# Global value rows of batch 1 written by VectorE; casts of batch 2's global rows placed behind batch 1's first pair

## The chip, the cores and the metric

The kernel runs on one core of one Trainium2 chip. The metric is the device time of one execution in microseconds (us); the figure for a kernel is the median of several runs. Engines are named as in the profile: PE is TensorE, DVE is VectorE, ACT is ScalarE, POOL is GpSimd, SP is SyncE, which issues most transfers.

## What is computed

A sliding-window attention with eight global tokens, and behind it a two-layer expert with a squared Relu:

```python
def _attn_ref(q, k, v, global_idx):          # q, k, v: 8 batches, 8 heads, 576 tokens, 64
    scores = scale * np.matmul(q, k.transpose(0, 1, 3, 2))
    mask = np.abs(pos[:, None] - pos[None, :]) <= 32
    mask = mask | is_global[:, None] | is_global[None, :]   # 8 global tokens
    scores = np.where(mask, scores, -1000000000.0)
    attn = softmax(scores)
    return np.matmul(attn, v)

def _moe_ref(x, w_in, w_out):                # x: 4608 x 512, w_in: 512 x 2048
    h = x @ w_in
    r = np.maximum(h, 0.0)
    return (r * r) @ w_out
```

Inputs and output are float32; the kernel computes in float16 with float32 sums.

## The kernel before

**Attention.** The heads of a batch are taken in four pairs, so that there are 32 pairs in all (`unit(i, ...)`, i = 4 * batch + pair). The 576 tokens stand in five key tiles of 120 tokens, and in front of each tile's tokens stand the eight global keys, so a tile has 128 rows. A pair is worked in two halves of its queries (`half`): scores (L617), Exp on ScalarE (L626), a multiplication with the mask on VectorE (L629), and the matmuls with the values (L653, L662), whose sums are divided (Ln and Exp of the negative, L685 and L686) and written into `xT` (L715), from which the expert reads. What the global queries add up to is kept apart (`gsh`, L703) and is spread over the eight global columns of `xT` by eight small copies per batch (`scatter`, L734).

**Value tiles.** `vb0` and `vb1` hold the values of even and odd batches. In partitions 0 to 7 of each of the five tiles stand the value rows of the global tokens (`vb[b][0:NG, x, ...]`), in the partitions behind them the tokens' rows, which POOL's queue fetches (`fetch_values`, L113). The global rows get there in three ways: for batch 0 VectorE casts them from `gv0` and copies them five times (`v_globals`, L447 and L449); for batches 1 and 2 VectorE casts both batches' rows at once into `g16s["v"]` (`values_in_place`, L368), and SP issues five transfers per batch from there (`value_globals`, L431); from batch 3 on they come from a gather through device memory (`gscr`). The float32 rows for batches 0 to 2 were fetched by SP at the start (`fetch_globals`, `grows`).

**Queries and keys.** Those of batches 0 and 1 are transposed on TensorE (`tr_k`, `tr_q`, L458 to L500). From batch 2 on they are laid out in scratch memory (`scr_k`, `scr_q`): tokens by nine transfers of POOL (`tokens_to_scratch`, L410), the eight global rows by one transfer each of SP (`globals_to_scratch`, L391; for batch 2 from `g16s["k"]` and `g16s["q"]`, which VectorE casts in `next_in_place`, L376). Two transposing transfers of SP bring them into `kb` and `qb` (`transposes`, L422). A one-element copy into `pin` on POOL (L846 for batch 2) holds POOL's token transfers back until something of the batch before has been written.

**Order.** There is no scheduler: each engine runs its instructions in the order in which the code records them, and SP and POOL issue transfers in that order too. Expert work stands in a list, `queue`, as pieces: `mm1_half` and `mm1` (L533, L514; a Relu, and a square on VectorE, L545 and L520) and `mm2` (L577; an evacuation L554 and an output store L556). `take(n)` records the next n pieces; `unit` does so between its own steps, after the scores, between the halves and at the end. In batch 1 a unit also transposes the next pair.

Around the change the order is: the last work of batch 0, `scatter(0, 1)`, `values_in_place()`, the rest of the queue, then everything that prepares batch 2, then the four units of batch 1. Each transfer and each reader of a tile waits for what the tile framework finds it to depend on.

Of the kernel before, what the change touches and what calls it, by code (L numbers as in the profile page):

```python
# [9 lines left out]
FP16 = mybir.dt.float16  # L10
# [37 lines left out]
def kernel(  # L48
# [11 lines left out]
    B, H, S, D = q.shape  # L60
    NG = global_idx.shape[0]
# [16 lines left out]
    def sbt(name, shape, dtype, bufs=1, tag=None):  # L78
        return sb.tile(shape, dtype, name=name, tag=(tag or name), bufs=bufs)
# [8 lines left out]
    pool, dve, act = nc.gpsimd, nc.vector, nc.scalar  # L88
# [5 lines left out]
    vb = {0: sbt("vb0", [P, NT, 2 * H, D], FP16)}  # L94
    w_in = sbt("w_in", [P, NDM, dff], FP16)
    w_out = sbt("w_out", [P, NFF, dm], FP16)
    XOFF = 36
    xT = sbt("xT", [P, NDM, XOFF + B * S], FP16)
# [13 lines left out]
    def fetch_values(b, x, hs=slice(0, H)):  # L112
        pool.dma_start(  # L113
            out=vb[b][NG : NG + KN[x], x, 2 * hs.start : 2 * hs.stop : 2],
            in_=v[b, hs, x * KT : x * KT + KN[x]].rearrange("h s d -> s h d"),
        )
# [44 lines left out]
    rows = sbt("rows", [P, 2], FP16)  # L161
# [25 lines left out]
    def clear_ones(op, t, tiles=range(NT)):  # L187
        for x in tiles:
            op(t[:, x, 1 : 2 * H : 2].bitcast(FP32), ONES)
# [144 lines left out]
    def gathered(nm, b):  # L334
        n = NG * H
        return gst[(nm, b // 2 - 1)][(b % 2) * n : (b % 2) * n + n]
# [3 lines left out]
    def store_rows(nm, b):  # L340
        gscr[(nm, b)] = dram.tile([NG, H * D], FP16, name=f"gscr_{nm}{b}")
        nc.sync.dma_start(
            out=gscr[(nm, b)].rearrange("g (h d) -> (g h) d", d=D), in_=gathered(nm, b)
        )

    grows = sbt("grows", [NG, 7, H, D], FP32, bufs=2, tag="gt")
    grow = {nm: grows[:, 2 * i : 2 * i + 2] for i, nm in enumerate("kqv")}
    gv0 = grows[:, 6]
    g16s = {nm: sbt("g16s" + nm, [NG, 2, H, D], FP16) for nm in "kqv"}

    def fetch_globals():
        _, at = nc.values_load_multi_w_load_instructions(
# [11 lines left out]
                    in_=src[nm][1:3, :, ds(at[g], 1), :].rearrange("b h o d -> o b h d"),  # L364
                )

    def values_in_place():
        dve.tensor_copy(out=g16s["v"], in_=grow["v"])  # L368
        value_globals(1)

    def globals_in_place(nm):
        act.copy(out=nat[nm][TP : TP + NG, :, TJ - 1], in_=grow[nm][:, 0])

    def next_in_place():
        for nm in "kq":
            dve.tensor_copy(out=g16s[nm][:, 1], in_=grow[nm][:, 1])  # L376

    def globals_to_scratch(b):
        for nm in "kq":
            rows, n, pitch, off = {"k": (KW, NT, P, 0), "q": (QW, 4, GRP, GTOK)}[nm]  # L380
            if (nm, b % 2) not in scr:
                scr[(nm, b % 2)] = dram.tile([rows, H * D], FP16, name=f"scr_{nm}{b % 2}")
                if nm == "k":
                    nc.sync.dma_start(
                        out=scr[("k", b % 2)][(NT - 1) * P + 8 + KN[-1] : KW],
                        in_=idle[0 : P - 8 - KN[-1]],
                    )
            t = scr[(nm, b % 2)]
            dst = t.rearrange("(x r) (h d) -> x r h d", x=n, d=D)[:, off : off + NG]
            if b == 2:  # L390
                nc.sync.dma_start(  # L391
                    out=dst.rearrange("x g h d -> g x (h d)"),
                    in_=g16s[nm][:, 1].rearrange("g h d -> g (h d)").unsqueeze(1).to_broadcast(
                        (NG, n, H * D)
                    ),
                )
                continue
            nc.sync.dma_start(
                out=dst.rearrange("x g h d -> (g h) x d"),
                in_=gathered(nm, b).unsqueeze(1).to_broadcast((NG * H, n, D)),  # L400
            )
        if b > 2:
            store_rows("v", b)

    def tokens_to_scratch(b):
        for nm in "kq":
            n, step, pitch, off = {"k": (NT, KT, P, NG), "q": (4, GTOK, GRP, 0)}[nm]
            for x in range(n):
                lo, hi = x * step, min((x + 1) * step, S)
                pool.dma_start(  # L410
                    out=scr[(nm, b % 2)][x * pitch + off : x * pitch + off + hi - lo].rearrange(
                        "s (h d) -> s h d", d=D
                    ),
                    in_=src[nm][b, :, lo:hi].rearrange("h s d -> s h d"),
                )

    def transposes(b):
        for nm, d_, w in (("k", kb, KW), ("q", qb, QW)):
            if not d_:
                d_["all"] = sbt(nm + "b", [P, 2, NHP, w], FP16, tag="st" + nm)  # L420
            d_[b] = d_["all"][:, b % 2]
            nc.sync.dma_start_transpose(out=d_[b], in_=scr[(nm, b % 2)][:, :])  # L422

    def values(b):
        t = vb[b]
        for x in range(NT):
            fetch_values(b, x)

    def value_globals(b):
        for x in range(NT):  # L430
            nc.sync.dma_start(  # L431
                out=vb[b][0:NG, x, 0 : 2 * H : 2],
                in_=gscr[("v", b)].rearrange("g (h d) -> g h d", d=D)
                if b > 2
                else g16s["v"][:, b - 1],
            )

    def cast_tokens(op, nm, hp):
# [4 lines left out]

    gv16 = sbt("gv16", [NG, H, D], FP16)

    def v_globals():
        dve.tensor_copy(out=gv16, in_=gv0)  # L447
        for x in range(NT):
            dve.tensor_copy(out=vb[0][0:NG, x, 0 : 2 * H : 2], in_=gv16)  # L449

    def transposed(nm, i, tag):
        b, hp = divmod(i, NHP)
# [143 lines left out]
    def take(n):  # L596
        for _ in range(min(n, len(queue))):
            fn, a = queue.pop(0)
            fn(*a)

    gsum = {}
    pin = sbt("pin", [P, 1], FP32)
# [8 lines left out]
    def scores(i, half, tag, wins):  # L611
        kt, qt = key_query(i)
        sc = pst(tag, [P, 2, 512])
        for t, so, c0, w in wins[half]:
            for e in range(2):
                r = slice(64 * e, 64 * e + 64)
                nc.tensor.matmul(  # L617
                    sc[:, e, so : so + w], kt[r, t, :], qt[r, c0 : c0 + w],
                    start=True, stop=True, skip_group_check=True,
                )  # L620
        return sc

    def weights(half, sc, wins):
        W = sum(x[3] for x in wins[half])
        et = sbt("et", [P, 2, SCW[0]], FP16, bufs=4)
        act.activation(  # L626
            out=et[:, :, 0:W], in_=sc[:, :, 0:W], func=AF.Exp, bias=0.0, scale=scale
        )
        dve.tensor_tensor(  # L629
            out=et[:, :, 0:W], in0=et[:, :, 0:W],  # L630
            in1=mask[:, MB[half] : MB[half] + W].unsqueeze(1).to_broadcast((P, 2, W)),
            op=ALU.mult,
        )
        return et
# [94 lines left out]
    def scatter(b, part=None, pairs=slice(0, NHP)):  # L729
        lo, hi = {  # L730
            None: (XOFF + b * S, XOFF + (b + 1) * S), 0: (0, HS + 1), 1: (XOFF, XOFF + S),
        }[part]
        for g in range(NG):
            dve.tensor_copy(  # L734
                out=xT[:, pairs, lo:hi][:, :, ds(gvs[part][g], 1)],
                in_=gxs[b][:, pairs, g : g + 1],
            )
# [29 lines left out]
    def half0(i):  # L767
        tag = pair_tag[i % 2]
        ets[i] = weights(0, scores(i, 0, tag, WIN), WIN)
# [26 lines left out]
        fetch_values(1, x)  # L796
    for j in range(4):
        pool.dma_start(out=w_out[:, ts(j, 4), :], in_=wo[:, ts(j, 4), :])
    v_globals()
    half0(2)  # L800
    keep_warm(SCHED["w6"])
    half0(3)
# [36 lines left out]
    tr_k(NHP, tag="tr")  # L839
    tr_q(NHP, tag="mm", op=act.copy)  # L840
    scatter(0, 1)
    values_in_place()
    take(99)
    next_in_place()
    globals_to_scratch(2)
    pool.tensor_copy(out=pin[0:1], in_=xT[0:1, 0, XOFF + 256 : XOFF + 257])  # L846
    tokens_to_scratch(2)
    transposes(2)
    vb[2] = vb[0]
    values(2)  # L850
    value_globals(2)
    queue += units[1] + units[2]

    def unit(i, n, nxt=None):
        scs = [scores(i, half, pair_tag[half], WIN2) for half in range(2)]
        et = [weights(half, scs[half], WIN2) for half in range(2)]
        take(n[0])
        if nxt:
            tr_k(nxt, tag="tr", tail=act.copy)
            tr_q(nxt, tag="mm", op=act.copy)  # L860
        for half in range(2):
            acc = outputs(i, half, et[half], pair_tag[half], WIN2, columns=i < 2 * NHP)
            finish_outputs(i, half, acc, columns=i < 2 * NHP)
            if half == 0:
                take(n[1])
        if i % NHP == NHP - 1:
            scatter(i // NHP)
        take(n[2])

    for hp in range(NHP):  # L870
        unit(NHP + hp, SCHED["b1"][hp], NHP + hp + 1 if hp + 1 < NHP else None)
        if hp == 2:
            clear_ones(dve.memset, vb[0])
            index_base()
# [51 lines left out]
```

## Time and profile before

| | us |
|---|---|
| median of 7 runs | 334.35 |
| lowest, highest | 334.0, 335.47 |
| profiled execution, its own time | 334.32 |
| span of the profiled execution | 332.5 |
| PE, busy in the span | 318.9 (96%) |
| DVE, busy | 228.8 (69%) |
| ACT, busy | 210.9 (63%) |
| POOL, busy | 106.5 (32%) |

Batch 0 takes the span up to about 34, batch 1 runs from there to 73, and batches 2 to 7 follow at about 33 each; the rest is expert work alone. The profile is of one execution. Its page gives busy time per engine, the span in 40 slices, queues, the chain of work that ended last, and groups of instructions by line and tile; the trace behind it can be asked for the order of instructions on an engine, with the idle time before each and what ended that.

### The profile page before, as it was taken

To read this page: it belongs to the slowest core of one execution; us is meant where nothing else is said; L and a number is where in the kernel's file an instruction comes from. 1 tells how busy PE (TensorE), PEld (TensorE's weight loads), DVE (VectorE), ACT (ScalarE), POOL (GpSimd) and SP (SyncE) were. 2 spreads that over 40 slices of the span, in tenths; PEclk is the share of its full clock that TensorE was granted. 3 is DMA by queue.
4 is the path that set the end of the run, shared out by engine and by line. 5 is a ranking of instruction groups with operands and counts; after the bars stand their busy time and mean duration, and the time that the engine had idled before them with its cause. 6 is when DMAs were issued, how large, how long until landed. Compare 5 with 4: busy or idle time off the path is not lost.

```text
span 332.5 us, 6922 instructions
## 1 busy us (share of the span) xinstructions
PE 318.9 (96%) x2427; PEld 166.0 (50%) x2427; DVE 228.8 (69%) x678; ACT 210.9 (63%) x416; POOL 106.5 (32%) x138
## 2 busy tenths in 40 slices
PE   8899489999999999999999999999999999999995
PEld 3558366545445454545454545454544444444444
DVE  7787936788868875888588858885888585323421
ACT  3879436559954995499549954995499536404700
POOL 9734635008940590059305900590000000000000
PEclk9999959999999999999999999999999999999999
DMA  8999999935999699489966998899710001011012
GB/s 182 178 204 181 173 188 143 157 110 72 149 140 134 99 144 153 117 109 135 138 137 101 144 143 124 110 146 122 138 65 0 34 32 64 2 63 63 2 53 73
DMA packets 148716, 37.59 MB, mean 113 GB/s; under 512 B 136658, under 2 KB 144202, under 8 KB 148682
## 3 DMA queue, kind: packets, MB, share of 16 engines
q0 software_dynamic: 105168, 17.93, 74.2%
q1 hardware_dynamic: 43368, 19.10, 31.4%
q8 instruction: 19, 0.31, 0.4%
q14 instruction: 15, 0.12, 0.2%
q10 hardware_dynamic: 146, 0.13, 0.1%
HBM read 37.31 MB, written 17.05 MB: 164 GB/s over the span
## 4 chain that ended last, share of the span: by engine, by line
PE 82%; DVE 7%; DMA 4%; ACT 3%; issue 2%; SPq 2%; DVEq 0%
PE mm L577 26%; PE mm L514 25%; PE tr L514 9%; PE tr L577 6%; PE mm L533 3%; PE sc L662 3%; PE acc L662 3%; PE sc L617 2%; DVE xT L734 2%; PE acc L617 2%; DMA vb<-g16sv 2%; DMA grows<-in_v_dram 2%; SPq L357 2%; ACT rec L686 1%; DVE xT L715 1%
## 5 line engine op out<-in xcount | busy, mean ns | idle before, releaser
L577 PE MATMUL mm<-w_out,gt 128*128 128x512 f16 x448 | 104.4, 379 | 0.0
L514 PE MATMUL mm<-xT,w_in 128*128 128x512 f16 x384 | 90.1, 379 | 0.8 <-DVE xT L734 0.8
L577 PEld LDWEIGHTS <-gt 128*128 128x128 f16 x560 | 52.5, 98 | 58.7
L514 PEld LDWEIGHTS <-w_in 128*128 128x128 f16 x512 | 47.5, 98 | 53.9 <-issue 1.0
L519 ACT ACTIVATE rl<-mm 128x512 f16<-128x512 f32 x96 | 54.8, 600 | 26.0 <-PE mm L514 25.3
L520 DVE TENSOR_TENSOR gt<-rl 128x512 f16<-128x512 f16 x128 | 52.1, 423 | 16.7 <-ACT rl L519 14.5
L626 ACT ACTIVATE et<-sc 128x880 f16<-128x880 f32 (+1 forms) x32 | 28.9, 902 | 45.1 <-PE sc L617 45.1
L629 DVE TENSOR_TENSOR et<-et,mask 128x880 f16<-128x880 f16 (+1 forms) x64 | 38.8, 613 | 23.3 <-ACT et L626 23.1
L113 POOL DMA_DIRECT2D vb<-in_v_dram x40 | 40.4, 1507 | 8.5 <-DMA w_in<-in_moe_w_in_dram 7.3
L514 PE MATMUL tr<-xT,w_in 128*128 128x512 f16 x128 | 33.0, 380 | 0.0
L554 DVE COPY ot<-mm 128x512 f32<-128x512 f32 (+1 forms) x29 | 19.7, 680 | 17.5 <-PE mm L577 15.8
L715 DVE TENSOR_TENSOR xT<-sc,rec 64x288 f16<-64x288 f32 (+1 forms) x55 | 25.0, 455 | 7.1 <-ACT rec L686 6.6
L686 ACT ACTIVATE rec<-rec 128x288 f32<-128x288 f32 x64 | 28.3, 443 | 2.0
L626 ACT ACTIVATE et<-acc 128x880 f16<-128x880 f32 (+1 forms) x32 | 29.0, 906 | 0.0
L662 PEld LDWEIGHTS <-vb 128*128 128x128 f16 x288 | 21.2, 98 | 12.8 <-issue 2.1
L715 DVE TENSOR_TENSOR xT<-acc,rec 64x288 f16<-64x288 f32 (+1 forms) x55 | 25.0, 455 | 3.7 <-ACT rec L686 0.9
L410 POOL DMA_DIRECT2D scr_k<-in_k_dram x30 | 26.5, 1070 | 2.8 <-issue 2.4
L685 ACT ACTIVATE rec<-sc 64x288 f32<-64x288 f32 (+1 forms) x55 | 22.3, 406 | 7.6 <-PE sc L662 4.2
L410 POOL DMA_DIRECT2D scr_q<-in_q_dram x24 | 24.6, 1544 | 5.9 <-DMA w_out<-in_moe_w_out_dram 5.9
L577 PE MATMUL tr<-w_out,gt 128*128 128x512 f16 x112 | 25.3, 379 | 0.0
L884 POOL COPY pin<-gsh 1x1 f32<-1x1 f32 x5 | 0.9, 187 | 71.4 <-DVE gsh L703 71.4
L685 ACT ACTIVATE rec<-acc 64x288 f32<-64x288 f32 (+1 forms) x55 | 22.2, 404 | 1.7 <-PE acc L653 0.9
(143 smaller groups left out, 303.3 us busy)
## 6 DMA issues: line engine op xcount, KB each, us to landing
out_dram<-ot SPq DMA_DIRECT2D x35, 256.0 KB
vb<-in_v_dram POOLq DMA_DIRECT2D x32, 120.0 KB, 11.1
scr_q<-in_q_dram POOLq DMA_DIRECT2D x24, 144.0 KB, 6.1
scr_k<-in_k_dram POOLq DMA_DIRECT2D x24, 120.0 KB, 4.8
w_in<-in_moe_w_in_dram POOLq DMA_DIRECT2D x4, 512.0 KB, 11.9
w_out<-in_moe_w_out_dram POOLq DMA_DIRECT2D x4, 512.0 KB, 11.2
natk<-in_k_dram POOLq DMA_DIRECT2D x3, 288.0 KB, 14.9
natq<-in_q_dram POOLq DMA_DIRECT2D x3, 288.0 KB, 11.3
```

Of the source, the lines that this page charges most:

```text
L113: pool.dma_start(out=vb[b][NG : NG + KN[x], x, 2 * hs.start : 2 * hs.stop : 2], in_=v[b, hs, x * KT : x * KT + KN[x]].rearrange("h s d -> ...
L410: pool.dma_start(out=scr[(nm, b % 2)][x * pitch + off : x * pitch + off + hi - lo].rearrange("s (h d) -> s h d", d=D), in_=src[nm][b, :, l ...
L514: nc.tensor.matmul(ph, w_in[:, t, u * P : (u + 1) * P], xT[:, t, XOFF + c * TC : XOFF + (c + 1) * TC], start=(t == 0), stop=(t == NDM - 1),)
L519: nc.scalar.activation(out=rl, in_=ph, func=AF.Relu)
L520: nc.vector.tensor_tensor(out=gts[c][:, u, :], in0=rl, in1=rl, op=ALU.mult)
L577: nc.tensor.matmul(po, gts[c][:, f, m * P : (m + 1) * P], w_out[:, f, :], start=(f == 0), stop=(f == NFF - 1),)
L626: act.activation(out=et[:, :, 0:W], in_=sc[:, :, 0:W], func=AF.Exp, bias=0.0, scale=scale)
L629: dve.tensor_tensor(out=et[:, :, 0:W], in0=et[:, :, 0:W], in1=mask[:, MB[half] : MB[half] + W].unsqueeze(1).to_broadcast((P, 2, W)), op=AL ...
L662: nc.tensor.matmul(banks[e][:, o : o + w], vtf[:, t, vo : vo + P], et[:, e, so : so + w], start=(n == 0), stop=(n == nw - 1), skip_group_c ...
L685: act.activation(out=rec[r], in_=av[xs][rs, :, 0:GTOK], func=AF.Ln)
L686: act.activation(out=rec, in_=rec, func=AF.Exp, scale=-1.0)
L715: dve.tensor_tensor(out=xT[r, hp, x0 : x0 + HS].rearrange("p (k x) -> p k x", k=2), in0=av[x][r, :, 0:GTOK], in1=rec[r], op=ALU.mult,)
```

## The change

`values_in_place` goes. For batch 1 the function that wrote batch 0's global value rows is called with batch 1's rows: VectorE casts 8 x 512 elements into `gv16` and copies them five times into `vb1`, and no transfer is issued. `g16s` holds one batch instead of two. The casts of batch 2's k and q rows, and now of its v rows as well, are recorded behind the first unit of batch 1 instead of before it, and with them all transfers for batch 2: SP's into scratch, its transposes and value rows, and POOL's token transfers with the copy into `pin`.

```diff
-    g16s = {nm: sbt("g16s" + nm, [NG, 2, H, D], FP16) for nm in "kqv"}
+    g16s = {nm: sbt("g16s" + nm, [NG, H, D], FP16) for nm in "kqv"}
...
-    def values_in_place():
-        dve.tensor_copy(out=g16s["v"], in_=grow["v"])
-        value_globals(1)
...
     def next_in_place():
-        for nm in "kq":
-            dve.tensor_copy(out=g16s[nm][:, 1], in_=grow[nm][:, 1])
+        for nm in "kqv":
+            dve.tensor_copy(out=g16s[nm], in_=grow[nm][:, 1])
...
-                else g16s["v"][:, b - 1],
+                else g16s["v"],
...
-    def v_globals():
-        dve.tensor_copy(out=gv16, in_=gv0)
+    def v_globals(b, rows):
+        dve.tensor_copy(out=gv16, in_=rows)
         for x in range(NT):
-            dve.tensor_copy(out=vb[0][0:NG, x, 0 : 2 * H : 2], in_=gv16)
+            dve.tensor_copy(out=vb[b][0:NG, x, 0 : 2 * H : 2], in_=gv16)
...
-    v_globals()
+    v_globals(0, gv0)
...
     scatter(0, 1)
-    values_in_place()
+    v_globals(1, grow["v"][:, 0])
     take(99)
-    next_in_place()
-    globals_to_scratch(2)
-    pool.tensor_copy(out=pin[0:1], in_=xT[0:1, 0, XOFF + 256 : XOFF + 257])
-    tokens_to_scratch(2)
-    transposes(2)
-    vb[2] = vb[0]
-    values(2)
-    value_globals(2)
     queue += units[1] + units[2]
...
     for hp in range(NHP):
         unit(NHP + hp, SCHED["b1"][hp], NHP + hp + 1 if hp + 1 < NHP else None)
+        if hp == 0:
+            next_in_place()
+            globals_to_scratch(2)
+            pool.tensor_copy(out=pin[0:1], in_=xT[0:1, 0, XOFF + 256 : XOFF + 257])
+            tokens_to_scratch(2)
+            transposes(2)
+            vb[2] = vb[0]
+            values(2)
+            value_globals(2)
         if hp == 2:
```

More of the change, by code (lines that the diff above doesn't have):

```diff
@@ L392, in globals_to_scratch @@
                     out=dst.rearrange("x g h d -> g x (h d)"),
-                    in_=g16s[nm][:, 1].rearrange("g h d -> g (h d)").unsqueeze(1).to_broadcast(
+                    in_=g16s[nm].rearrange("g h d -> g (h d)").unsqueeze(1).to_broadcast(
                         (NG, n, H * D)
```

## The prediction

> **What bounds the kernel now.** I read the slices of the page first, then TensorE's own order of instructions around the one dip that they show, then the engines and queues that feed that place. All times are us from the start of the span.
>
> Busy tenths and granted clock, in 40 slices of 8.3 us:
>
> ```profile
> PE   8899489999999999999999999999999999999995
> PEclk9999959999999999999999999999999999999999
> ```
>
> TensorE is full everywhere from the third slice on, except in slice 5 (33 to 42), and in the slice behind it the clock is halved. Whatever frees TensorE there moves the end; elsewhere hardly anything does. TensorE's order at that place (start, duration, line, count, idle time before it and what ended that):
>
> ```profile
> 37.64 0.43 PE L462 MATMUL mm<-identity,natq 96*64 96x96 f16 x12
> 41.94 0.26 PE L653 MATMUL sc<-et,vb 128*64 128x160 f16 x2 [3.88 <-DVE kt L490]
> ...
> 42.69 0.37 PE L653 MATMUL sc<-et,vb 128*64 128x192 f16 x2 [0.42 <-DMA vb<-g16sv]
> ...
> 43.62 1.89 PE L533 MATMUL mm<-xT,w_in 128*128 128x256 f16 x8
> ...
> 46.31 4.16 PE L533 MATMUL mm<-xT,w_in 128*128 128x256 f16 x24
> 50.41 0.36 PE L617 MATMUL sc<-qt,kt 64*128 64x160 f16 x6
> ```
>
> The first pair of batch 1 stands still for 3.88 before its first value matmul. The name "kt L490" is only the last event before the start: in the program that weight load waits for the first of the five `vb<-g16sv` transfers, and the trace's landing records put them at 41.81, 42.55, 43.20, 44.00 and 44.73. The same stretch in sums:
>
> ```profile
> 38.00:42.33 4.33, 0.39 (x8) 0.17 (x4) 3.54 (x9) 0.92 (x4) 2.49 (x3) 1.00 1.28 206
> 42.33:49.10 6.77, 6.30 (x42) 4.13 (x43) 2.68 (x9) 2.30 (x5) 2.36 (x3) 0.50 1.72 190
> ```
>
> (length; busy of PE, weight loads, DVE, ACT, POOL; granted clock; DMA share; GB/s.) After the stall the clock is 0.50 for 6.77 us, so 24 matmuls take 4.16 there; at 31.46 the same 24 took 2.79. The stall costs twice.
>
> VectorE before the stall:
>
> ```profile
> 35.64 0.68 DVE L368 CAST g16sv<-grows 8x1024 f16<-8x1024 f32 x1 [0.19 <-issue]
> ...
> 37.97 0.41 DVE L376 CAST g16sk<-grows 8x512 f16<-8x512 f32 x1
> 38.30 0.78 DVE L376 CAST g16sq<-grows 8x512 f16<-8x512 f32 x1
> 39.01 1.12 DVE L629 TENSOR_TENSOR et<-et,mask 128x880 f16<-128x880 f16 x2
> ```
>
> The masked weights of half 0 are there at about 39.57 and those of half 1 at 40.13, well ahead of the rows. SP's queue:
>
> ```profile
> 36.35 3.83 SPq L431 DMA_DIRECT2D vb<-g16sv  x5
> ...
> 40.81 0.28 SPq L391 DMA_DIRECT2D scr_k<-g16sk  x1
> ...
> 52.34 5.84 SPq L422 DMA_TRANSPOSE kb<-scr_k  x1
> 58.42 6.93 SPq L422 DMA_TRANSPOSE qb<-scr_q  x1
> ```
>
> The k transpose starts when the last token rows of `scr_k` land (52.06); the q transpose follows it on SP and lands at 68.78. Its first reader:
>
> ```profile
> 73.01 0.36 PE L617 MATMUL sc<-qb,kb 64*128 64x160 f16 x6
> ...
> 74.10 1.89 PE L514 MATMUL mm<-xT,w_in 128*128 128x512 f16 x8 [0.54 <-DVE xT L734]
> ```
>
> So batch 2 has 73.01 - 68.78 = 4.23 in hand, and no more.
>
> **The change part by part.**
>
> *Five transfers go, VectorE writes the rows.* The nearest rows are batch 0's, the same code:
>
> ```profile
> 15.24 0.41 DVE L447 CAST gv<-grows 8x512 f16<-8x512 f32 x1 [0.65 <-DMA grows<-in_k_dram]
> 15.69 1.09 DVE L449 COPY vb<-gv 8x512 f16<-8x512 f16 x5
> ```
>
> Start to start that is 0.45 + 1.02 = 1.47, in place of 0.61 (35.64 to 36.25): +0.86. The k and q casts leave this place: 37.97 to 39.01, -1.04. The mask of half 0 then starts at about 38.85 and ends at 39.4. The token rows of vb1 landed by 37.91, so the mask is what is late next, and the value matmuls start at 39.5: idle 1.44 in place of 3.88 (-2.44), and the 0.42 goes (-0.42).
>
> *The clock.* An idle of 0.76 at 35.5 left the clock at 1.00, one of 3.88 did not; 1.44 is nearer the former, so I take full clock. At full clock (rows at 53.29, 54.74 and 31.46) the stretch is shorter by: first outputs 1.26 to 0.49 (0.77), 8 matmuls 1.82 to 0.92 (0.90), second outputs 0.87 to 0.51 (0.36), 24 matmuls 4.10 to 2.75 (1.35); sum 3.38. With 2.86 from above that is 6.24. ScalarE takes some of it back: the last of those units needs a PSUM bank that ScalarE empties behind its q copies (end 42.26), Ln, Exp and Relu, some 1.3 later, about 0.3 after TensorE wants it. The next pair's scores then start at 44.5 instead of 50.41: -5.9.
>
> *Three casts behind the first pair.* VectorE still has a Relu (0.68) and three squares (0.42 each) from that pair when they come: the squares end at about 46.6. The casts cost 1.1 (two at 0.41 and overlap) to 2.3 (three at 0.78); I take 1.3, nearest to the measured pair of casts (1.04). The next masks start at 47.9 and TensorE, which wants the first at 47.5, gets it at 48.5: +1.0, so its outputs are at 48.5 instead of 53.29 (-4.8). Behind them the copies of `kt` and the sums of that pair are late by some 0.7 against TensorE, and in before the scores of the following pair start at 58.33, just as VectorE lets their bank go (58.27): +0.6. Batch 2's scores would be wanted at 73.01 - 4.2 = 68.8.
>
> *What is moved past which queue.* POOL: nothing is passed. In the built program its order is the same, and the copy into `pin` that releases the token rows waits for the same scatter (end 35.45). SP: five issues (3.83) go, but the transfer of k rows into `scr_k` now waits for a cast that ends at about 47.0 instead of 38.4, and queued behind it stand the q rows, both transposes, the value rows of batch 2 and four output stores. Issue to landing of that transfer was 5.0 (40.81 to 45.81); bounds are 2.2 (the k rows of batch 3, 78.12 to 80.34, on quiet DMA engines) and 6.8 (the last fetch of global rows, 27.75 to 34.56). At 5.0, the nearest, k rows land at 52.1, level with the tokens (52.06): the transposes stay where they are. Bounds 49.3 and 53.9: nothing to +1.8. The removed transfers are 320 short packets of 28,182 between 30 and 75, 0 to 0.5 earlier for the tokens. So `qb` lands between 68.3 and 70.6, most likely at 68.9.
>
> *Sum.* Wanted at 68.8, there at 68.9: gain 4.1. The next matmuls (74.10) wait for the scatter anyway, which hides a few tenths more of lateness. Value rows of batch 2 land at 69.04 to 71.18, and their readers (75.82 and 77.07) move to 71.7 and 73.0. Batch 3 and all later ones are triggered by the first pair of the batch before them and move along; its q rows had 1.7 in hand (105.13 to 106.82). The profiled execution took 334.32 (span 332.5 and 1.8 around it) and the median is 334.35, so 334.3 - 4.1 = 330.2.
>
> **A rule against the change.** While VectorE cast q rows at 38.30 (0.78, twice k's 0.41), POOL issued token transfers at 0.90 each, no slower than the 0.88 to 0.93 at 42.82 and later, when VectorE was idle. The Trainium skill, "SBUF — State Buffer", on its two separate sides, says that a VectorE copy in a two-port mode and GpSimd lock each other out of a shared port pair, and that POOL's descriptors starve meanwhile. By it, the new 1.5 us of copies would delay POOL's issues, the transposes and the end by up to 1.5: 331.7. The rows show the cost on VectorE, not on POOL, so my sum holds none of that.
>
> **Rivals.**
> *The clock falls all the same.* For: 1.44 idle plus gaps in the pair's matmuls. Against: the 0.76 gap. The stretch keeps its 3.38, the k cast ends at about 50.0, its rows land at 55.0 and `qb` at 71.7: gain 1.3, 333.0.
> *Slower: VectorE's new copies are held up while POOL issues.* For: the q cast's 0.78 beside POOL's issues. Against: the five at 15.69 took 0.27 to 0.30 each with POOL issuing until 15.90. At 0.78 each they cost 3.9, the mask ends at 42.5, TensorE stalls as before and the clock falls; the casts come behind the square that ended at 51.57, k rows land at 57.0, `qb` at 73.7, and the casts themselves hold the next masks: +0.9, 335.2. It decides from copies of some 3.2 in all, when the first pair gains under 0.7 and k rows land after 52.06 + 4.23 = 56.3.
> *The rows still come by transfer.* The built program excludes it: the weight loads of batch 1 wait for VectorE and the tokens alone.
>
> **How the numbers follow.** A measurement of this kernel tells about 0.2% (0.7 us) from no change; the seven runs span 334.0 to 335.47. The forecast, gains of 2.4 (k rows at 6.8) to 5.2 (casts hidden, tokens 0.5 earlier), has 0.76; the falling clock 0.12; no visible change 0.03; slower 0.09. The range goes from 329.1 to the falling clock's 333.0.
>
> **What would show it.** Right: no `vb<-g16sv` before 65; idle of 1 to 2 before L653's twin at about 39.5, PEclk 9 in every slice, next scores near 44.5; the k transpose still at 52 to 53; batch 2's scores at 69, with TensorE waiting there for `qb` under 1 us. Wrong: clock 0.50 after 42, or single copies over 0.5, or a k transpose after 54, or a batch 3 that waits for its own rows.

## The result and the profile after

The changed kernel takes 331.05 us (median of 14 runs, 329.56 to 334.42) against 334.66 for the kernel before (35 runs). The ratio of the means is 0.9902, with a 95% interval from 0.9884 to 0.992: 3.3 us faster, between 2.7 and 3.9; the medians lie 3.6 apart. The forecast was 330.2, a gain of 4.1. Repeated beside later experiments the same kernel gave 0.9926 (0.9904 to 0.9949). Line numbers of the changed kernel are four lower than before from the transposes on (L653 is L649, L629 is L625, L422 is L418).

These are the slices of the page after. In this execution there is no half clock left, and the dip of TensorE in slice 5 is smaller:

```profile
PE   8889699999999999999999999999999999999996
PEclk9999999999999999999999999999999999999999
```

TensorE's order in batch 1 and at the start of batch 2:

```profile
39.60 0.45 PE L458 MATMUL mm<-identity,natq 96*64 96x96 f16 x12 [1.31 <-ACT rl L540]
40.83 0.26 PE L649 MATMUL sc<-et,vb 128*64 128x160 f16 x2 [0.78 <-DVE et L625]
...
42.82 2.99 PE L529 MATMUL mm<-xT,w_in 128*128 128x256 f16 x24
45.75 0.36 PE L613 MATMUL sc<-qt,kt 64*128 64x160 f16 x6
...
49.67 0.26 PE L649 MATMUL sc<-et,vb 128*64 128x160 f16 x2 [0.76 <-DVE et L625]
...
55.12 0.37 PE L613 MATMUL acc<-qt,kt 64*128 64x112 f16 x6 [0.41 <-DVE xT L711]
...
69.79 0.36 PE L613 MATMUL sc<-qb,kb 64*128 64x160 f16 x6
...
70.89 1.89 PE L510 MATMUL mm<-xT,w_in 128*128 128x512 f16 x8 [0.55 <-DVE xT L730]
```

No wait for a transfer is left in batch 1. The stall of 3.88 has become two: 1.31 for a bank of PSUM (the memory that takes TensorE's sums), which ScalarE empties with a Relu, and 0.78 for the mask. Both end on VectorE's queue, the first because that Relu itself waited 2.15 for VectorE's squares:

```profile
38.95 1.09 ACT L540 ACTIVATE rl<-mm 128x512 f16<-128x512 f32 x2 [2.15 <-DVE gt L541]
```

The 24 matmuls take 2.99 instead of 4.16. All later waits of batch 1 name VectorE as well. Batch 2's first scores do not wait.

VectorE in the same stretch:

```profile
36.12 0.41 DVE L443 CAST gv<-grows 8x512 f16<-8x512 f32 x1 [0.19 <-issue]
36.57 1.96 DVE L445 COPY vb<-gv 8x512 f16<-8x512 f16 x5
...
40.17 1.14 DVE L625 TENSOR_TENSOR et<-et,mask 128x880 f16<-128x880 f16 x2
...
47.64 0.41 DVE L372 CAST g16sk<-grows 8x512 f16<-8x512 f32 x1
47.97 0.41 DVE L372 CAST g16sq<-grows 8x512 f16<-8x512 f32 x1
48.31 0.79 DVE L372 CAST g16sv<-grows 8x512 f16<-8x512 f32 x1
```

The five copies take 1.96, where batch 0's took 1.09. In the trace the single ones take 0.28, 0.27, 0.64, 0.27 and 0.79. POOL is issuing the token transfers just then, from 36.61 on. Its third and fourth issue take 1.07 and 1.19 against 0.90 for its first, but they take as much in move_only below, where no such copies run. SP's queue:

```profile
48.07 0.29 SPq L387 DMA_DIRECT2D scr_k<-g16sk  x1
...
52.85 6.25 SPq L418 DMA_TRANSPOSE kb<-scr_k  x1
59.34 6.41 SPq L418 DMA_TRANSPOSE qb<-scr_q  x1
```

The k rows land at 52.77 and the transpose starts behind them, as forecast. But `qb` lands at 67.67, 2.1 ahead of its reader.

### The profile page after: what moved, and what is told of

Read it like the earlier page. It is cut to its first block, busy times and chain, and to the rows that moved or that the text cites. A ratio compares the mean times of both kernels' runs of the same rounds, so it can differ in the third digit from the quotient of the medians.

```text
span 329.1 us, 6919 instructions
## 1 busy us (share of the span) xinstructions
PE 316.7 (96%) x2427; PEld 165.0 (50%) x2427; DVE 230.7 (70%) x684; ACT 210.3 (64%) x416; POOL 106.6 (32%) x138
## 4 chain that ended last, share of the span: by engine, by line
PE 78%; DVE 11%; ACT 5%; issue 2%; DMA 2%; SPq 2%; DVEq 0%
PE mm L510 25%; PE mm L573 25%; PE tr L510 9%; PE tr L573 6%; PE sc L658 3%; PE acc L658 3%; PE sc L613 2%; DVE xT L730 2%; SPq L357 2%; ACT rec L682 2%; ACT rec L681 2%; PE acc L613 2%; DMA grows<-in_k_dram 1%; DVE xT L711 1%; DVE gt L541 1%
## 5 line engine op out<-in xcount | busy, mean ns | idle before, releaser
L625 DVE TENSOR_TENSOR et<-et,mask 128x880 f16<-128x880 f16 (+1 forms) x64 | 38.8, 613 | 22.4 <-ACT et L622 22.2
L658 PEld LDWEIGHTS <-vb 128*128 128x128 f16 x288 | 21.2, 98 | 12.8 <-issue 2.1
```

The source lines that it names most:

```text
L625: dve.tensor_tensor(out=et[:, :, 0:W], in0=et[:, :, 0:W], in1=mask[:, MB[half] : MB[half] + W].unsqueeze(1).to_broadcast((P, 2, W)), op=AL ...
L658: nc.tensor.matmul(banks[e][:, o : o + w], vtf[:, t, vo : vo + P], et[:, e, so : so + w], start=(n == 0), stop=(n == nw - 1), skip_group_c ...
```

## The experiments

The work in front of batch 1 ends at a slightly different time in each execution. So the profiles are compared by one distance: from VectorE's first cast of value rows for batch 1 to the first scores of batch 2. It ends where the rest of the kernel begins.

The granted clock differs from one execution to the next as well, and its mean over the span is on record for each. Half of 3.41 is 0.5% of a span of 329, so one stretch of 3.41 at half clock leaves a mean of 0.995, as in the profile of after_again, and one of 6.83 leaves 0.990, as in the profile of the kernel before. The last column counts the executions with a mean of 0.998 or more, which leaves no room for such a stretch. For the kernel before it counts the 44 executions whose clock is on record.

| kernel | distance, us | median, us | ratio to before (95%) | executions at 0.998 or more |
|---|---|---|---|---|
| before | 37.37 | 334.66 | | 0 of 44 |
| the change | 33.67 | 331.05 | 0.9902 (0.9884 to 0.992) | 8 of 14 |
| the change, again | 34.19 | 331.54 | 0.9926 (0.9904 to 0.9949) | 3 of 6 |
| rows_only | 34.44 | 332.71 | 0.9942 (0.9918 to 0.9967) | 1 of 11 |
| move_only | 36.63 | 334.36 | 1.0011 (0.9989 to 1.0032) | 0 of 11 |
| warm_before | 34.96 | 332.58 | 0.995 (0.9935 to 0.9966) | 8 of 8 |
| pin_late | 32.72 | 330.08 | 0.988 (0.9854 to 0.9906) | 4 of 4 |
| second_pair | 33.53 | 330.53 | 0.988 (0.9862 to 0.9898) | 2 of 5 |
| casts_mid | 33.52 | 329.22 | 0.9847 (0.9828 to 0.9866) | 4 of 5 |
| three_edits | 31.44 | 329.29 | 0.9857 (0.9835 to 0.9879) | 4 of 4 |
| values_third | 32.04 | 329.18 | 0.9852 (0.9836 to 0.9868) | 5 of 5 |
| four_edits | 31.67 | 328.43 | 0.9828 (0.9809 to 0.9848) | 5 of 5 |

**rows_only**: the value rows by VectorE, the rest in its old place.

```diff
 (on the changed kernel)
     take(99)
+    next_in_place()
+    globals_to_scratch(2)
+    ...
+    value_globals(2)
     queue += units[1] + units[2]
...
-        if hp == 0:
-            next_in_place()
-            ...
```

> The first part of the change alone: VectorE writes batch 1's global value rows, but the three casts and everything that prepares batch 2 stay in front of batch 1. Theory (the gain is the stall of TensorE and the halved clock behind it; the place of the casts only shifts VectorE's queue): the casts of 1.1 to 1.5 us return in front of the first masks, the first value matmuls start 1.1 to 1.5 later than in the changed kernel, at about 42, without the half clock, and the casts are gone from the second pair, which gives about 0.8 back. End 331 to 332, gain over before 2.5 to 3.5. If the clock falls after the longer idle, 333.5 to 334.5. Rival (the gain comes from moving the preparation out of the way): no gain, 334 to 335.

It gained 0.58% (1.5), between the first expectation and the one with a falling clock. TensorE waited 1.32 for ScalarE and then, with the casts in front of the masks again,

```profile
41.58 0.34 PE L649 MATMUL sc<-et,vb 128*64 128x160 f16 x2 [1.85 <-DVE et L625]
```

and in this execution the clock was at 0.50 from 41.17 to 44.59. The second pair's masks were not waited for. So writing the rows on VectorE gains by itself, about half of what the change gains; the rival, under which it would bring nothing, falls.

Moving the casts adds the rest, and the record shows that it goes with the clock. The one execution of rows_only at full clock took 329.99, no more than the change's eight (329.56 to 331.15); the other ten, at 0.989 to 0.995, took 331.39 to 333.40. That the clock holds more often in the change because its wait for the masks is shorter (0.78 instead of 1.85) is likely, but no run shows it apart from the rest.

**move_only**: the transfers stay, the rest is moved behind the first pair. The diff is the change's last two hunks without `v_globals(1, ...)`.

> The second part alone: batch 1's rows still come by five transfers, but the casts of k and q and all that prepares batch 2 are recorded behind the first pair. Theory: TensorE still stalls until the rows land at about 41.5 and the clock falls; k rows are cast near 52, land near 57, the transposes start 4 to 5 later than before, q rows land at 73 to 74 and TensorE waits for them: 334.5 to 335.7, no gain or slower. Rival (the move brings the gain): about 331.

There was no difference (0.9989 to 1.0032), as expected, but not for the expected reason. The stall was there (3.98), and the k rows were cast at 50.58. SP's queue then:

```profile
51.01 0.28 SPq L391 DMA_DIRECT2D scr_k<-g16sk  x1
...
55.73 4.21 SPq L422 DMA_TRANSPOSE kb<-scr_k  x1
60.18 3.50 SPq L422 DMA_TRANSPOSE qb<-scr_q  x1
```

The first transpose started 3.4 later than in the kernel before and both together took 7.7 instead of 12.8; `qb` landed at 65.60, not at 73 to 74. The late k rows cost nothing here; the stall and the half clock (6.83) were still there.

**warm_before**: the kernel before, with the idle time filled by matmuls of zeros.

```diff
 (on the kernel before, in unit)
             tr_q(nxt, tag="mm", op=act.copy)
+        if i == NHP:
+            w = pst("acc", [P, 2, 512])
+            for _ in range(15):
+                nc.tensor.matmul(w[:, 0], idle[:, 0:P], idle, start=True, stop=True)
```

> The kernel before with 15 matmuls of zeros (128x512) recorded between the transposes and the first value matmuls of batch 1's first pair; their result is not used. The rows still come by transfer and land at about 41.8. Theory: the idle time is filled, the granted clock stays at 1.00, the stretch from 42 to 50 is shorter by 3.4 less 0.3 for ScalarE, the second pair's scores start at 47 to 47.5, and batch 2's scores near 70: 331 to 332, a gain of 2.5 to 3, that is most of the change's gain with the stall itself still there. Rival (the waiting itself is what costs, or the half clock is not due to the idle time): 334 to 335.

```profile
38.55 3.41 PE L864 MATMUL acc<-idle 128*128 128x512 f16 x15
42.35 0.26 PE L653 MATMUL sc<-et,vb 128*64 128x160 f16 x2 [0.39 <-DMA vb<-g16sv]
...
43.18 0.27 PE L653 MATMUL sc<-et,vb 128*64 128x192 f16 x2 [0.49 <-DMA vb<-g16sv]
...
43.93 0.23 PE L653 MATMUL sc<-et,vb 128*64 128x88 f16 x2 [0.39 <-DMA vb<-g16sv]
```

The clock stayed at 1.00 and the kernel gained 0.5% (1.7), half of the change's gain, with the transfers still in it. It is less than the 2.5 to 3 expected: at full clock TensorE reaches the second and third tile before their rows and waits 0.49 and 0.39 for them, 0.88 in place of 0.42, time that the half clock had covered. The terms "clock" and "wait for rows" overlap and must not be added whole.

**pin_late**: POOL issues its token transfers behind VectorE's copies.

```diff
 (on the changed kernel)
-            pool.tensor_copy(out=pin[0:1], in_=xT[0:1, 0, XOFF + 256 : XOFF + 257])
+            pool.tensor_copy(out=pin[0:1], in_=vb[1][0:1, NT - 1, 0, 0:1])
```

> The changed kernel, but POOL's token transfers for batch 2 wait until VectorE has written the last of batch 1's global value rows, about 2 us later. Theory (two of the five copies took 0.64 and 0.79 instead of 0.27 because POOL was issuing transfers at that time): the five copies take 1.1 in all instead of 1.96, the first value matmuls start 0.8 earlier, and since tokens then land little later the end is 0.3 to 0.8 earlier than the changed kernel: 330.3 to 330.8. Rival (the copies are slow by themselves, or the wait for the tokens decides): copies still 1.9, time 331 or, if the transposes start 2 later and TensorE waits for them, 331 to 331.5.

```profile
35.51 1.09 DVE L445 COPY vb<-gv 8x512 f16<-8x512 f16 x5
...
37.67 0.45 PE L458 MATMUL mm<-identity,natq 96*64 96x96 f16 x12 [0.17 <-ACT rl L540]
```

The same five copies in the same place take 1.09 once POOL is not issuing beside them (its first issue starts at 37.26), and the wait of TensorE for ScalarE shrinks from 1.31 to 0.17. The distance is 0.95 shorter. That the copies were held up by POOL's issues is thereby shown; the gain in time, 331.05 or 331.54 to 330.08, agrees, though it is not shown, since the intervals overlap.

**second_pair**: casts and preparation behind the second pair of batch 1 (`if hp == 1`).

> The changed kernel with the casts and everything that prepares batch 2 recorded behind the second pair of batch 1 instead of the first: k rows are cast near 54 instead of 47.6, and SP's transposes cannot start before their rows have landed, near 59. Theory (what the DMA engines still have to move sets when q rows land, not when the first transpose starts): issues of 4.2 and 3.5 us as in move_only, q rows land at 68.5 to 70, TensorE waits 0 to 0.6 for them: 330.7 to 331.7, as the changed kernel. Rival (each us that the k rows come later moves the transposes and q rows by one us, as the prediction priced it): issues of 6.3 and 6.4, q rows at 74, TensorE waits 4: 335 to 336.

```profile
59.84 2.97 SPq L418 DMA_TRANSPOSE kb<-scr_k  x1
63.05 2.76 SPq L418 DMA_TRANSPOSE qb<-scr_q  x1
```

The first transpose starts 7.0 later than in the changed kernel, and `qb` lands at 67.85 against 67.67. The expected issues were still too long; the verdict is plain all the same: between 52 and 60, when the transposes start does not decide when they end. The value tokens of batch 2, which land beside the transposes in the change, had all landed by 58.61 here. The masks of the second pair are free of casts, and the kernel is no slower than the change (0.988).

**after_again, casts_mid, three_edits, four_edits, values_third.** These ask what bounds the changed kernel. casts_mid records the casts inside the first pair, behind its transposes; three_edits adds pin_late and moves the copies of tiles 3 and 4 behind the first masks; four_edits and values_third add a later start of batch 2's value tokens.

```diff
 (three_edits, on the changed kernel, beside the line of pin_late;
  v_globals now takes the tiles as a third argument;
  casts_mid is the move of next_in_place() alone)
-    v_globals(1, grow["v"][:, 0])
+    v_globals(1, grow["v"][:, 0], range(3))
...
     et = [weights(half, scs[half], WIN2) for half in range(2)]
+    if i == NHP:
+        v_globals(1, grow["v"][:, 0], range(3, NT))
     take(n[0])
     if nxt:
         tr_k(nxt, tag="tr", tail=act.copy)
         tr_q(nxt, tag="mm", op=act.copy)
+    if i == NHP:
+        next_in_place()
...
         if hp == 0:
-            next_in_place()
...
 (four_edits: hp == 1 and pair 1; values_third: hp == 2 and pair 2)
-            values(2)
             value_globals(2)
+        if hp == 2:
+            pool.tensor_copy(out=pin[0:1], in_=gsum[1][0:1, 0, 2, 0, 0:1])
+            values(2)
```

> The changed kernel unchanged, as the measure for the three below. Every theory: 330.5 to 331.5, about 0.99 of before; first value matmuls of batch 1 near 40.8, two long copies among the five, q rows landed about 2 us ahead of TensorE's first use of them.

> The changed kernel with the three casts of batch 2's k, q and v rows recorded inside batch 1's first pair, between its transposes and its value matmuls, where VectorE waits for ScalarE for some 1.3 us. Theory (VectorE's queue in front of the second pair's masks holds TensorE): the wait for the second pair's masks (0.76) goes, most of the 0.4 behind it too, 0.6 to 1.0 earlier than the changed kernel: 330.0 to 330.5. Rival (the rows for scratch and the transposes set the end): no change in batch 2's start, 331.

> Three edits on the changed kernel: the casts inside the first pair as in casts_mid, POOL's tokens held until the last copy of value rows as in pin_late, and the copies for tiles 3 and 4, which only the second half reads, recorded behind the first pair's masks. Theory: masks another 0.4 earlier than in pin_late and the casts hidden; TensorE would want batch 2's q rows at about 66.3, while they landed at 67.3 to 67.7 in the changed kernel and in pin_late, so here the transfers become the bound for the first time: 329 to 329.8, with TensorE waiting up to 1 us for q rows. Rival (queues still elsewhere): as pin_late, 330.

> three_edits, and batch 2's value token transfers on POOL recorded behind the second pair and held until that pair's first sums, so that they no longer run beside the two transposes. In move_only the transposes started at 55.7 and their issue took 4.2 and 3.5 us instead of 5.8 to 6.3 and 6.4 to 7.1. Theory (the value tokens slow the transposes): issue of the transposes 4 to 5 us each, q rows land at 64 to 65.5, the wait for them goes, 0.5 to 1 less than three_edits: 328.3 to 329. Rival (the transposes are slow for another reason, or the value tokens become late): q rows no earlier, or batch 2's value matmuls wait; time as three_edits or worse.

> three_edits, with batch 2's value token transfers held until the third pair's first sums (near 57) instead of the second pair's as in four_edits. Theory (the two transposes share the DMA engines with whatever else is queued there, so the last of them lands when the engines run dry, at 66.5 to 67.7 in every run so far that started the first at 52 to 53): without the value tokens before 57 the k transpose lands by 60 and q rows by 64 to 65.5, TensorE no longer waits for them; the value tokens land near 67 to 68, ahead of their readers at 70: 328 to 328.7. Rival (the transposes' own length decides): q rows again at 66.6 to 67.7 and the time of four_edits, 328.4, or worse if the value tokens become late.

In casts_mid the second pair's masks start without delay and the time falls to 0.9847, clear of after_again's interval, so the casts in VectorE's queue had cost time. Its gain in time (2.3) is larger than the 0.67 by which its profile's distance is shorter than after_again's. Both profiles have the clock at 0.50 for 3.41, from 40.4 and 40.6, but the profiled execution of casts_mid was the slowest of its five (330.56); the other four kept the clock and took 328.84 to 329.55. In after_again the executions that kept it took 331.17 to 331.70 and those with one such stretch 331.20 and 331.50. So the clock does not explain the whole difference, and what made the rest is open. second_pair has the same distance as casts_mid (33.53): with one stretch it took 330.53 to 330.86, without it 329.80 and 330.24. The medians of these kernels thus differ in part by how often the clock fell.

three_edits has the shortest distance, TensorE reaching batch 2 at 67.01 just behind `qb` at 66.85. Against casts_mid its time does not differ. In four_edits the transposes still took 5.09 and 7.40 and `qb` landed at 67.05, so the expectation for them failed: the value tokens, issued from 51.76 instead of 50.72, still ran beside them. In values_third they were issued from 58.30:

```profile
52.70 3.89 SPq L418 DMA_TRANSPOSE kb<-scr_k  x1
56.83 3.30 SPq L418 DMA_TRANSPOSE qb<-scr_q  x1
```

`qb` lands at 63.71 and the tokens at 62.76 to 66.38. That is close to the expectation of values_third for the transposes, though not for the time (329.18). POOL's later issues now ran beside VectorE's small index instructions: three of them, from 60.64 on, took 0.41, 0.60 and 0.47, where four_edits has 0.10, 0.23 and 0.17, and TensorE waited 0.90 instead of 0.29 for the fourth pair's masks behind them. four_edits is the fastest kernel measured, 328.43, 1.7% under the kernel before; its interval overlaps those of casts_mid, three_edits and values_third.

## Why the prediction was right, and where its steps were not

The forecast gain was 4.1; 3.3 was measured, the profile's distance shrank by 3.70, and faster was the right sign for the right cause.

**The stall and the clock: right in kind.** The transfers were what TensorE waited for, and the half clock behind the stall was half of what was gained (warm_before). "I take full clock" held in the profile of the change and in 8 of its 14 executions. In the profile of after_again the clock fell for 3.41 all the same, as the first rival had it:

```profile
PEclk9999989999999999999999999999999999999999
```

The distance was 0.52 longer there. Part of the loss was covered: TensorE, at half clock, no longer waited for the second pair's masks, which had cost it 0.76. Five executions of the change had a mean clock of 0.993 to 0.995 and took 331.47 to 331.94, about 1.0 above the median of the eight that kept the clock (330.56); in after_again one stretch made no difference. One execution of each fell further, to 0.988 and 0.990, and took 334.42 and 333.26, 3.9 and 1.7 above the executions that kept the clock. The rival had priced the whole fall at 2.8, which lies between those two; the half of it, which came more often, cost 0 to 1.0. The forecast had no term for executions in which the clock falls.

**The copies: mis-sized.** The step "1.47 in place of 0.61: +0.86" took batch 0's rows, where POOL had one issue beside them. What was measured is 2.34 (36.12 to 38.46), so +1.73. The slower rival had named the mechanism and set its point at copies of 3.2 in all; 1.96 stayed under it. With the different start of the two executions taken out (0.48), the first value matmuls came at 40.35 instead of the forecast 39.5.

**A chain not seen.** The squares behind the copies come later, ScalarE's Relus wait for their buffers, and TensorE's q transposes wait for the PSUM bank (1.31). The prediction had looked at the mask alone as what is late next.

**The casts: right.** 1.3 forecast, 1.38 measured (47.64 to 49.02); masks waited for by 0.76, and 0.41 at the next pair's bank.

**The gate of `qb`: wrong.** "Nothing to +1.8" for the k rows and "`qb` lands between 68.3 and 70.6, most likely at 68.9" put the limit there. It landed at 67.67, ahead of all of that, and limited nothing. (The upper bound for the k rows also misread an issue: the last fetch of global rows starts at 27.91, so it took 6.65, not 6.8.) The step that failed is the one that moves the end of the transposes with their start: move_only started them 3.4 later than the kernel before and second_pair 7.0 later than the change, and `qb` landed 3.2 earlier and 0.2 later. What moved the end was the traffic beside them: with the value tokens held back in values_third, `qb` landed at 63.71. The slower rival's price (`qb` at 73.7) rested on the same step. The two wrong terms, an optimistic arrival at 68.8 (69.31 with the start taken out) and a gate at 68.9, nearly agree. That is chance, and it made the sum look safer than it was.

**The rule that was weighed.** The Trainium skill, "SBUF — State Buffer", on its two separate sides, has VectorE's two-port copies and GpSimd lock each other out. pin_late agrees in kind: copies of 0.64 and 0.79 against 0.27. Not every copy beside an issue was held up, though: the first two ran within POOL's first issue (36.61 to 37.51) and took 0.28 and 0.27. The prediction's reading by that rule, POOL late and the transposes with it, is not how the cost reached the end; it came over VectorE's queue. The row "0.90 each" that the prediction set against it is four issues in 3.61; beside the q cast the single ones took 1.07 and 0.98. That alone does not show POOL held up either, since issues of 1.07 and 1.19 stand in move_only with no copy of global rows beside them.

## What to carry to other kernels

A short transfer in front of a busy matmul engine can cost twice, as here, by its landing time and by the clock behind the stall; a few copies on an engine that is at hand can replace it, if they do not run beside POOL's issues. When a wait is removed, follow every reader of the engine that takes over the work, and not only the one that waited before. Two waits that lie in one stretch are not added: let each cover the other once, and see what is left. Where the clock holds in some executions and falls in others, read it for each execution before two medians are compared.

## What the runs showed of the hardware

- The half clock in batch 1 came in lengths of 6.83 (before, move_only) and 3.41 (rows_only, after_again, second_pair, casts_mid), after an idle time of 3.88 or 3.98 in the former and of two waits, 1.31 or 1.32 and 0.78 to 1.85, in the latter. The Trainium skill, "TensorE: Matmul & The Clock Gate", Part 1, gives a free-running window of 3.4 us; these lengths are one and two of it. After the same waits of 1.31 and 0.78 the same kernel had the half clock in one profile and not in another.
- Issuing the two transposes took 11.6 to 13.5 of SP's time in the nine profiles with value tokens queued beside them (12.7 in the change), and 5.7 and 7.2 where the tokens had landed before (second_pair) or were issued later (values_third). The Trainium skill, "DMA: Bandwidth & Descriptors", on queues, rings and completion order, says that an engine takes its queues in turn by the packet. The runs agree with that in the sum alone.
- Five transfers of 8 KB between two places in on-chip memory took 5.2 to 5.5 us from issue to landing while the DMA engines were loaded with weights (36.35 to 41.81 for the first).
- Short VectorE instructions on 8 partitions were stretched beside POOL's issues of transfers: two of five copies from 0.27 to 0.64 and 0.79 (the change), one cast from 0.41 to 0.79 (48.31, beside an issue from 47.84 to 48.85).
